# Summing the convolution taps of the first two blocks on TensorE, and taking the first unit's weights first

## Chip, cores and metric

The kernel runs on one core of one Trainium2 chip. The metric is the device time of one execution in microseconds. The kernel before was run three times: 1166.29, 1167.04 and 1167.16 us, median 1167.04 us.

## The reference

```python
# x [2, 4096, 192], weight_gen [2, 4096, 8, 7]; everything in fp32
w = softmax(weight_gen, axis=-1)                 # 7 taps for each token and head
x_pad = concat([zeros(B, 6, D), x], axis=1)
out[b, s, h, g] = sum_k w[b, s, h, k] * x_pad[b, s + k, h, g]     # h: 8 heads of 24 columns
y = out.reshape(8192, 192)
h = y @ moe_w_in;   y = maximum(0.01 * h, h) @ moe_w_out           # [192, 2048], [2048, 192]
h = y @ moe2_w_in;  y = where(h > 0, h, exp(min(h, 0)) - 1) @ moe2_w_out
```

## The kernel before

The 8192 tokens are cut into 16 blocks of 512. For each block three stages follow one another: a causal convolution with softmax weights (`conv_block`), a first feed-forward layer (l = 0) and a second (l = 1). Each layer has 2048 hidden columns, worked on as 8 **units** of 256. Of a unit, `ins` multiplies the block by 256 columns of the first weight matrix into a PSUM tile `h` (two buffers), `elementwise` makes the activation and splits it into a high part `gh` and a low part `gl` (ACT and DVE), and `outs`, four units later (LAG = 4), adds its product with the second weight matrix into the PSUM tile `acc`. All operands of the large matmuls are pairs of a high and a low part in fp32r, so every product is three matmuls. The two halves of the rows (0 to 63, 64 to 127) of TensorE are given separate matmuls, which run side by side.

Blocks 0 and 1 take turns, so the first four units are unit 0 of block 0, unit 0 of block 1, unit 1 of block 0 and unit 1 of block 1. These four only have their `ins` (`whole`, 9 steps of TensorE: 6 matmuls over all rows and 3 pairs); from the fifth unit on, one task `both` issues the `ins` of a unit and the `outs` of the unit four before it, and so on to the end.

The weights are made on the chip from 64-bit words (`split`): a DMA brings a piece (`load`, L213), ACT makes two intermediate values (`fraction`, L217, and `unbias`, L221), DVE joins them (`bits`, L228 and L231; `add`, L238), ACT writes the high part (`high`, L241) and DVE the low part (`low`, L246). Each unit needs its own pieces before its matmuls can start.

The convolution of one block: DMAs bring its weights (`load_w`, L288) and its tokens (`load_x`, L291). DVE and ACT make the softmax (`top`, `exp`, `total`, `scale`, L298 to L311). DVE then makes 7 products of tokens and weights (`mult`, L331, 128x768 each) and adds six of them to the first (`add`, L339). ACT writes the last 64 columns of each token twice (`double`, L374), TensorE transposes the block by matmuls with the identity (`transpose`, L388, 16 matmuls of 64x64), ACT writes the high part of the transposed block (L393) and DVE the low part (L396): that tile, `yt` or `xt`, is what the units multiply.

The order of every engine's work is fixed when the program is built. Each piece of work is a `Task` with a cost on one engine and a key; `Plan.order` plays the tasks through and, whenever an engine is free, gives it the ready task with the smallest key. Keys are counted in units of the steady run. The convolution of block 0 has an early key (`hurry` takes 12 off), and the first weights have the key of the unit that needs them. On the chip each engine then works its list off strictly in order.

Of the kernel before, what the change touches and what calls it, by code (L numbers as in the profile page):

```python
# [8 lines left out]
F32 = mybir.dt.float32  # L9
F32R = mybir.dt.float32r  # L10
I32 = mybir.dt.int32
U32 = mybir.dt.uint32
I64 = mybir.dt.int64
AF = mybir.ActivationFunctionType
ALU = mybir.AluOpType
AX = mybir.AxisListType

P = 128
D = 192
DFF = 2048  # L20
H = 8
K = 7
G = D // H
# [3 lines left out]
BS = 4  # L27
NB = SP // BS
N = BS * P
# [9 lines left out]

PACE = 0.28  # L40


# [88 lines left out]
def conv_moe_kernel(ctx: ExitStack, tc: tile.TileContext, x, wg, wi0, wi1, wo, out):  # L131
    nc = tc.nc

    rings = {
        "xs": (2, [P, BS + PAD, D], F32), "ws": (2, [P, BS * H, K], F32),
        "st": (1, [P, BS * H, 3], F32), "a": (1, [P, BS, D], F32), "prod": (1, [P, BS * D], F32),
        "xt": (1, [P, 4, N], F32R), "yt": (2, [P, 4, N], F32R),
        "h": (2, [P, 2, N], F32), "w": (3, [P, 2 * N], F32),
        "gh": (4, [P, 2 * N], F32R), "gl": (4, [P, 2 * N], F32R),
        "c": (1, [P, N], F32), "o": (1, [P, N], F32),  # L140
        "raw": (3, [P, 512], I64), "t": (2, [P, 512], I32),
    }
# [6 lines left out]
    plan = Plan({r: bufs for r, (bufs, _, _) in rings.items()})  # L149
# [18 lines left out]
    ident = const.tile([P, P], F32, name="ident")  # L168
    spare = const.tile([P, 1], F32, name="spare")
    win = {}  # L170
# [15 lines left out]
    bank = {p: acc[n % 2] for n, p in enumerate(phases)}  # L186
# [74 lines left out]
    def first(l, u):  # L261
        return min(at[l, i, u] for i in range(2))

    def split_in(l, part, m0, m1):
        c = slice(m0 // 2 * P, m1 // 2 * P) if part else slice(m0 * P, m1 * P)
        lo = [(win[l, part, 1][:, c], slice(None))]
        names = [("in", l, u) for u in range(m0 // 2, m1 // 2)]
        src = (wi0, wi1)[part][l][:, c]
        split(src, win[l, part, 0][:, c], lo, first(l, m0 // 2), names)

# [7 lines left out]
    xts = {}  # L278
    stored = {}

    def conv_block(i, due):
# [38 lines left out]
        prod = Slot("prod")  # L320
# [19 lines left out]

        y = [t, lx]
        for k in range(K):
            key = due - 0.8 - PACE * 2 * (K - 1 - k)
            takes = [[a], [prod]][k] if k < 2 else []
            uses = [r for r in [xs, ws, a] + [prod] * (k > 0) if r not in takes]
            y = [plan.add({"d": 0.95}, key, lambda k=k: mult(k), y, takes, uses)]
            if k:
                y = [plan.add({"d": 0.95}, key, add, y, uses=[a, prod])]
        last = y

        x_t = Slot("yt" if i < 2 else "xt")
        xts[0, i] = x_t

        place = Slot("h") if i == 2 else None

        def at_place():
            return place.tile if place else bank[0, i]

        def parts(j):

            return at_place()[:, :, j * N // 2 : (j + 1) * N // 2]

        def slot(j):
            return x_t.tile[:, j, :].rearrange("p (a b) -> p a b", a=2)

# [23 lines left out]

        def high(j):  # L390
            if not j:
                new(x_t)
            return nc.scalar.activation(slot(2 * j), parts(j), AF.Copy).ins  # L393

        def low(j):
            return nc.vector.tensor_tensor(  # L396
                out=slot(2 * j + 1), in0=parts(j), in1=slot(2 * j).bitcast(F32), op=ALU.subtract
            ).ins

        n = phases.index((0, i))  # L400
# [4 lines left out]

        k = due + (0.3 if i < 3 else 1.35)
        b = plan.add({"a": 0.55}, k, lambda: high(0), [t], [x_t], p)
        c = plan.add({"a": 0.55}, k + 0.1, lambda: high(1), [b], uses=[x_t] + p)
        b = plan.add({"d": 0.66}, k + 0.2, lambda: low(0), [b], uses=[x_t] + p)
        c = plan.add({"d": 0.66}, k + 0.3, lambda: low(1), [c], uses=[x_t] + p)  # L410
        return [b, c]

# [373 lines left out]
```

## Time and profile before

| | |
|---|---|
| median of 3 runs | 1167.04 us (1166.29 to 1167.16) |
| the profiled execution, its time | 1164.52 us |
| the profiled execution, its span | 1162.7 us |
| TensorE (PE) busy | 1119.4 us, 96% of the span |
| VectorE (DVE) busy | 808.2 us, 70% |
| ScalarE (ACT) busy | 788.3 us, 68% |
| PE busy in the first 52.43 us | 15.43 us |

The span is the part of the execution that the hardware profiler shows; the execution's own time is 1.8 us longer. Times in the views are counted from the start of the span. PE is the matmul row of TensorE, PEld its weight loads, POOL is GpSimd, SP the engine whose queue issues all DMAs. A busy PE is not a PE at its peak, since matmuls overlap each other.

### The profile page before, as it was taken

The numbers are of one execution on the slowest core, as the hardware profiler recorded it, in microseconds if no ns is written. First come the engines' busy times: TensorE is split into PE (matmuls) and PEld (weight loads), VectorE is DVE, ScalarE is ACT, GpSimd is POOL, SyncE is SP. The second block draws the span as 40 slices with busy tenths as digits, with TensorE's granted clock in tenths as the row PEclk, the third lists the DMA queues.
The fourth block names the chain that finished last, engine by engine and source line by source line (L and its number), as shares of the span: only waits on it lengthen the run. The fifth ranks groups of instructions, "written<-read, shape, count | busy, mean of one in ns | idle before, by whom it ended". The sixth has DMA issues, their size and how long they took to land.

```text
span 1162.7 us, 23771 instructions
## 1 busy us (share of the span) xinstructions
PE 1119.4 (96%) x9920; PEld 930.9 (80%) x9920; DVE 808.2 (70%) x1050; ACT 788.3 (68%) x1022; POOL 0.7 (0%) x6
## 2 busy tenths in 40 slices
PE   0699999999999999999999999999999999999998
PEld 0488998888888888888888888888888888888886
DVE  8999998948568494865948578494865839464464
ACT  1687898658586675857658576675857657585675
POOL 0000000000000000000000000000000000000000
PEclk9999999999999999999999999999999999999999
DMA  3424230000101001010100101001010000000000
GB/s 136 147 87 127 76 94 15 19 35 2 52 1 52 2 1 52 1 53 2 52 1 1 53 1 52 1 1 53 1 53 1 15 1 1 15 2 15 1 1 28
DMA packets 12620, 37.97 MB, mean 33 GB/s; under 512 B 1504, under 2 KB 3680, under 8 KB 12512
## 3 DMA queue, kind: packets, MB, share of 16 engines
q1 hardware_dynamic: 12512, 36.44, 9.8%
q8 instruction: 78, 1.28, 0.5%
q14 instruction: 30, 0.25, 0.1%
HBM read 30.15 MB, written 6.29 MB: 31 GB/s over the span
## 4 chain that ended last, share of the span: by engine, by line
PE 96%; DVE 3%; DMA 0%; ACT 0%; issue 0%; ACTq 0%; SPq 0%; DVEq 0%
PE acc L630 50%; PE h L630 45%; DVE prod L331 1%; DVE a L339 1%; PE acc L388 1%; DMA xs<-x_in 0%; ACT w L552 0%; DVE a L331 0%; DVE yt L396 0%; DVE t L231 0%; DVE w L563 0%; ACT yt L393 0%; DVE t L228 0%; DVE yt L440 0%; DVE c L425 0%
## 5 line engine op out<-in xcount | busy, mean ns | idle before, releaser
L630 PE MATMUL acc<-gh,wout 64*128 64x512 f32 (+1 forms) x3048 | 972.7, 386 | 0.0
L630 PE MATMUL acc<-gl,wout 64*128 64x512 f32 (+1 forms) x2032 | 785.5, 387 | 0.0
L630 PE MATMUL h<-yt,win 64*128 64x512 f32 (+1 forms) x2568 | 612.6, 389 | 18.5 <-ACT win L241 14.2
L630 PEld LDWEIGHTS acc<-gh,wout 64*128 64x128 f32 (+1 forms) x3048 | 560.1, 184 | 57.3
L630 PEld LDWEIGHTS h<-yt,win 64*128 64x128 f32 (+1 forms) x2568 | 470.2, 185 | 69.7 <-ACT win L241 14.3
L630 PE MATMUL h<-xt,win 64*128 64x512 f32 x2016 | 476.7, 386 | 0.1
L572 DVE TENSOR_TENSOR gl<-w,gh 128x1024 fp32r<-128x1024 f32 (+1 forms) x257 | 312.2, 1220 | 162.6 <-ACT gh L569 161.9
L630 PEld LDWEIGHTS acc<-gl,wout 64*128 64x128 f32 (+1 forms) x2032 | 374.1, 184 | 38.7 <-issue 0.4
L630 PEld LDWEIGHTS h<-xt,win 64*128 64x128 f32 x2016 | 370.6, 184 | 38.9 <-ACT gh L569 0.5
L569 ACT ACTIVATE gh<-w 128x1024 fp32r<-128x1024 f32 (+1 forms) x257 | 268.0, 1049 | 2.9
L552 ACT ACTIVATE w<-h 128x1024 f32<-128x1024 f32 x128 | 131.5, 1027 | 200.9 <-PE h L630 198.5
L563 DVE SCALAR_TENSOR_TENSOR w<-w,h 128x512 f32<-128x512 f32 x256 | 164.2, 683 | 141.4 <-ACT w L559 141.4
L555 ACT ACTIVATE w<-h 128x1024 f32<-128x1024 f32 x129 | 131.2, 1018 | 121.2 <-PE h L630 120.9
L559 ACT ACTIVATE w<-w 128x512 f32<-128x512 f32 x256 | 147.7, 624 | 3.9
L331 DVE TENSOR_TENSOR prod<-xs,ws 128x768 f32<-128x768 f32 x96 | 91.7, 955 | 1.9
L339 DVE TENSOR_TENSOR a<-a,prod 128x768 f32<-128x768 f32 x96 | 91.7, 955 | 1.5
L425 DVE TENSOR_TENSOR c<-acc,c 128x512 f32<-128x512 f32 (+1 forms) x32 | 22.0, 687 | 32.4 <-ACT o L455 23.6
L388 PE MATMUL acc<-ident,o 64*128 64x64 f32 x120 | 6.5, 231 | 19.6 <-ACT o L374 19.6
L388 PEld LDWEIGHTS acc<-ident,o 64*128 64x128 f32 x120 | 6.4, 147 | 21.6 <-issue 19.8
L418 ACT ACTIVATE c<-acc 64x512 f32<-64x512 f32 x32 | 19.1, 596 | 6.1 <-PE acc L630 5.2
L217 ACT ACTIVATE raw<-raw 128x384 int32<-128x384 uint32 (+3 forms) x30 | 17.2, 572 | 8.0 <-DMA raw<-wi_in 6.1
L231 DVE SCALAR_TENSOR_TENSOR t<-raw,t 128x384 int32<-128x384 int32 (+3 forms) x30 | 17.6, 585 | 1.0
(43 smaller groups left out, 257.8 us busy)
## 6 DMA issues: line engine op xcount, KB each, us to landing
xs<-x_in SPq DMA_DIRECT2D x16, 960.0 KB, 4.9
raw<-wo_in SPq DMA_DIRECT2D x16, 384.0 KB, 3.2
raw<-wi_in SPq DMA_DIRECT2D x10, 512.0 KB, 3.8
out_t<-o SPq DMA_DIRECT2D x16, 256.0 KB, 3.6
out_t<-c SPq DMA_DIRECT2D x16, 128.0 KB, 3.2
ws<-wg_in SPq DMA_DIRECT2D x16, 112.0 KB, 2.1
raw<-wi_in SPq DMA_DIRECT2D x2, 256.0 KB, 6.7
raw<-wi_in SPq DMA_DIRECT2D x1, 384.0 KB, 2.7
```

What stands on the lines that cost most here:

```text
L331: nc.vector.tensor_tensor(out=prods() if k else sums(), in0=xs.tile[:, k : BS + k, :].rearrange("p s (h g) -> p (s h) g", g=G), in1=ws.til ...
L339: nc.vector.tensor_tensor(out=sums(), in0=sums(), in1=prods(), op=ALU.add)
L388: nc.tensor.transpose(at_place()[:, half, c : c + 64], src, ident[r, r])
L418: nc.scalar.activation(new(c)[0:64], B[64:P], AF.Copy)
L425: nc.vector.tensor_tensor(out=c.tile[0:n], in0=B[0:n], in1=c.tile[0:n], op=ALU.add)
L552: nc.scalar.activation(cols(w), flat(), AF.Prelu, alpha=0.01)
L555: nc.scalar.activation(cols(w), flat(), AF.Relu, scale=-1.0)
L559: nc.scalar.activation(c, c, AF.Exp, scale=-1.0)
L563: nc.vector.scalar_tensor_tensor(out=c, in0=c, scalar=1.0, in1=h.tile[:, j, :], op0=ALU.subtract, op1=ALU.max,)
L569: nc.scalar.activation(cols(gh), cols(w), AF.Copy)
L572: return nc.vector.tensor_tensor(out=cols(gl), in0=cols(w), in1=cols(gh).bitcast(F32), op=ALU.subtract).ins
L630: i = nc.tensor.matmul(out_ap, w, x_ap, start=start, stop=stop).ins
```

## The change

For blocks 0 and 1 (ADDED = 2) the six additions on DVE, the doubling of the sum and the transposes of the sum are gone. Instead DVE writes each of the 7 products to a buffer of its own (`prod`, now 3 buffers), ACT writes the last 64 columns of each product twice (`dup`, 2 buffers), and TensorE multiplies every product by the identity in plain fp32 matmuls (not transposes) that accumulate over the 7 taps in PSUM: 16 matmuls for each tap, 112 for each block, 224 in all in place of 32 transposes. The high and low parts are then taken from PSUM as before (`splits`). Blocks 2 to 15 are computed as before.

The pieces of the first unit's first weight matrix get the key FIRST = -20.15, which places them ahead of the first block's products. The buffers for intermediate weights (`t`) go from 2 to 3. The scratch for DMAs described on the chip is set to 1024 bytes; no DMA of this kernel uses it.

```diff
-        "st": (1, [P, BS * H, 3], F32), "a": (1, [P, BS, D], F32), "prod": (1, [P, BS * D], F32),
+        "st": (1, [P, BS * H, 3], F32), "a": (1, [P, BS, D], F32), "prod": (3, [P, BS * D], F32),
...
-        "c": (1, [P, N], F32), "o": (1, [P, N], F32),
-        "raw": (3, [P, 512], I64), "t": (2, [P, 512], I32),
+        "dup": (2, [P, N], F32), "c": (1, [P, N], F32), "o": (1, [P, N], F32),
+        "raw": (3, [P, 512], I64), "t": (3, [P, 512], I32),
...
-        split(src, win[l, part, 0][:, c], lo, first(l, m0 // 2), names)
+
+        key = first(l, m0 // 2) if (l, m0) != (0, 0) else FIRST
+        split(src, win[l, part, 0][:, c], lo, key, names)
...
+        if i < ADDED:
+
+
+            def product(k, tap):
+                nc.vector.tensor_tensor(
+                    out=new(tap).rearrange("p (a g) -> p a g", g=G),
+                    in0=xs.tile[:, k : BS + k, :].rearrange("p s (h g) -> p (s h) g", g=G),
+                    in1=ws.tile[:, :, k : k + 1].to_broadcast([P, BS * H, G]),
+                    op=ALU.mult,
+                )
+
+            def doubled(tap, dup):
+                v = tap.tile.rearrange("p (s d) -> p s d", d=D)[:, :, P:D]
+                src = v.unsqueeze(2).to_broadcast([P, BS, 2, P // 2])
+                dst = new(dup).rearrange("p (s a b) -> p s a b", s=BS, a=2)
+                nc.scalar.activation(dst, src, AF.Copy)
+
+            def added(k, tap, dup):
+                for j in range(2):
+                    for s in range(BS):
+                        for half in range(2):
+                            r = slice(64 * half, 64 * half + 64)
+                            src = tap.tile[r, s * D : s * D + P]
+                            if j:
+                                src = dup.tile[r, s * P : (s + 1) * P]
+                            c = (j * BS + s) * 64
+                            nc.tensor.matmul(
+                                at_place()[:, half, c : c + 64], src, ident[r, r],
+                                start=k == j == s == 0,
+                                stop=(k, j, s) == (K - 1, 1, BS - 1),
+                            )
+
+            t = []
+            for k in range(K):
+                tap, dup = Slot("prod"), Slot("dup")
+                key = due - 0.8 - PACE * 2 * (K - 1 - k)
+                y = [plan.add({"d": 0.95}, key, lambda k=k, b=tap: product(k, b), y, [tap], [xs, ws])]
+                u = plan.add(
+                    {"a": 0.62}, key, lambda b=tap, d=dup: doubled(b, d), y, [dup], [tap]
+                )
+                t = [
+                    plan.add(
+                        {"pe": 1.2}, key, lambda k=k, b=tap, d=dup: added(k, b, d), [u] + t,
+                        uses=[tap, dup],
+                    )
+                ]
+            return splits(t[0], due + 0.3, [])
```

In the changed program the lines named above are L217 (load), L221 and L225 (fraction, unbias), L232 and L235 (bits), L242 (add), L245 (high), L250 (low), L304 to L317 (softmax), L361 and L364 (high and low part of the block), L383 (product), L394 (doubled), L405 (added), L610 to L630 (elementwise) and L688 (the units' matmuls).

The queue of DMAs (SP) is changed at its start: the two pieces for the first unit (256 and 128 columns) now stand directly behind block 0's softmax weights and ahead of block 0's tokens. Before, they stood behind the tokens of both blocks.

The rows below are in each engine's fixed order.

**VectorE (DVE), the first unit's weights.** Before, they stand inside block 1's convolution, around its last product (`a_105` is block 1's sum here):

```order
L331 TENSOR_TENSOR prod_109<-xs,ws 128x768
L339 TENSOR_TENSOR a_105<-a_105,prod_109 128x768
L228 TENSOR_SCALAR t<-t 128x128
L231 SCALAR_TENSOR_TENSOR t<-raw,t 128x128
L238 ISA t<-raw,t 128x512
L331 TENSOR_TENSOR prod_109<-xs,ws 128x768
L238 ISA t<-raw,t 128x256
L339 TENSOR_TENSOR a_105<-a_105,prod_109 128x768
L246 TENSOR_TENSOR win_71<-t,win_69 128x256
L246 TENSOR_TENSOR win_72<-t,win_70 128x128
```

Now they stand at the head of DVE's list, between the two halves of block 0's softmax:

```order
L232 TENSOR_SCALAR t<-t 128x256
L235 SCALAR_TENSOR_TENSOR t<-raw,t 128x256
L232 TENSOR_SCALAR t<-t 128x128
L235 SCALAR_TENSOR_TENSOR t<-raw,t 128x128
L242 ISA t<-raw,t 128x512
L242 ISA t<-raw,t 128x256
L312 TENSOR_REDUCE st_97<-ws 128x32
L313 TENSOR_SCALAR st_97<-st_97 128x32
L314 RECIPROCAL st_97<-st_97 128x32
L250 TENSOR_TENSOR win_71<-t,win_69 128x256
L250 TENSOR_TENSOR win_72<-t,win_70 128x128
L317 TENSOR_TENSOR ws<-ws,st_97 128x224
```

Everything that DVE does for the first unit's weights has moved from behind nearly all of both convolutions to ahead of block 0's first product.

**VectorE (DVE) around the low part of block 0** (`yt<-acc_79`), now; the first row is block 0's seventh product, the products behind it are block 1's:

```order
L383 TENSOR_TENSOR prod<-xs,ws 128x768
L317 TENSOR_TENSOR ws<-ws,st_97 128x224
L383 TENSOR_TENSOR prod<-xs,ws 128x768
L232 TENSOR_SCALAR t<-t 128x384
L235 SCALAR_TENSOR_TENSOR t<-raw,t 128x384
L383 TENSOR_TENSOR prod<-xs,ws 128x768 x2
L364 TENSOR_TENSOR yt<-acc_79,yt 128x512 x2
L383 TENSOR_TENSOR prod<-xs,ws 128x768 x3
```

Before, one product of block 1 stood ahead of the low part of block 0; now three stand there, and a piece of the second unit's weights.

**TensorE (PE) from block 0's last tap to the first unit** (`acc_79` is block 0's accumulator, `acc_80` block 1's; `h_366` is the first unit). Before, the transposes of block 0 stood directly ahead of the first unit:

```order
L388 MATMUL acc_79<-ident,o_139 128x64 x8
L388 MATMUL acc_79<-ident,a_105 128x64 x8
L630 MATMUL h_203<-yt,win_69 128x512
L630 MATMUL h_203<-yt,win_71 128x512
L630 MATMUL h_203<-yt,win_69 128x512 x2
```

Now:

```order
L405 MATMUL acc_79<-ident,prod 128x64 x8
L405 MATMUL acc_79<-ident,dup 128x64 x8
L405 MATMUL acc_80<-ident,prod 128x64 x8
L405 MATMUL acc_80<-ident,dup 128x64 x8
L405 MATMUL acc_80<-ident,prod 128x64 x8
L405 MATMUL acc_80<-ident,dup 128x64 x8
L405 MATMUL acc_80<-ident,prod 128x64 x8
L405 MATMUL acc_80<-ident,dup 128x64 x8
L688 MATMUL h_366<-yt,win_69 128x512
L688 MATMUL h_366<-yt,win_71 128x512
```

Three of block 1's seven taps stand between block 0's last tap and the first unit; the other four stand behind the first unit and ahead of the second.

## Rows read from the trace of the kernel before

**Rows 1.** The page: shares of the chain that ended last, by engine.

```profile
PE 96%; DVE 3%; DMA 0%; ACT 0%; issue 0%; ACTq 0%; SPq 0%; DVEq 0%
```

**Rows 2.** Stretches: start:end length, busy us (instructions) by engine, granted clock, DMA share, GB/s.

```profile
0.00:52.43 52.43, 15.43 (x81) 10.03 (x82) 45.95 (x78) 19.64 (x37) 0.70 (x6) 0.97 0.43 146
52.43:100.00 47.57, 47.57 (x426) 39.27 (x424) 44.71 (x70) 37.99 (x54) 0.00 (x0) 1.00 0.35 110
...
206.00:1157.60 951.60, 951.55 (x8496) 786.02 (x8492) 618.82 (x744) 637.39 (x796) 0.00 (x0) 1.00 0.06 19
```

**Rows 3.** PE's waits over the span: total us, times, longest us.

```profile
PE acc L388 <- ACT o L374: 19.6, 1, 19.6
PE h L630 <- ACT win L241: 14.2, 1, 14.2
```

**Rows 4.** Order of time, 0 to 24 us: start us, us, engine, instructions.

```profile
6.04 0.96 DVE L331 TENSOR_TENSOR a<-xs,ws 128x768 f32<-128x768 f32 x1 [0.42 <-DMA xs<-x_in]
...
9.33 0.44 ACT L217 ACTIVATE raw<-raw 128x256 int32<-128x256 uint32 x1 [5.17 <-DMA raw<-wi_in]
...
18.83 0.63 ACT L374 ACTIVATE o<-a 128x512 f32<-128x512 f32 x1 [8.00 <-DVE a L339]
...
19.60 0.69 PE L388 MATMUL acc<-ident,o 64*128 64x64 f32 x8 [19.60 <-ACT o L374]
...
20.76 1.09 ACT L393 ACTIVATE yt<-acc 128x512 fp32r<-128x512 f32 x2 [0.81 <-PE acc L388]
...
22.49 1.28 DVE L396 TENSOR_TENSOR yt<-acc,yt 128x512 fp32r<-128x512 f32 x2
```

**Rows 5.** The same view, 36 to 53 us.

```profile
36.70 4.08 PE L630 MATMUL h<-yt,win 128*128 128x512 f32 x11 [1.03 <-DVE win L246]
...
43.60 9.22 PE L630 MATMUL h<-yt,win 128*128 128x512 f32 x37 [2.21 <-DVE yt L396]
...
52.43 0.39 PE L630 MATMUL acc<-gl,wout 64*128 64x512 f32 x1
```

**Rows 6.** Groups by line and form, 0 to 52 us: count | busy us, mean ns.

```profile
L339 DVE TENSOR_TENSOR a<-a,prod 128x768 f32<-128x768 f32 x12 | 11.5, 958 | 0.4
...
L572 DVE TENSOR_TENSOR gl<-w,gh 128x1024 fp32r<-128x1024 f32 x2 | 2.4, 1218 | 0.2 <-ACT gh L569 0.2
...
L231 DVE SCALAR_TENSOR_TENSOR t<-raw,t 128x512 int32<-128x512 int32 x1 | 0.7, 691 | 0.0
```

**Rows 7.** Groups by line, DVE, 19.3 to 37 us: the first unit's pieces.

```profile
L231 DVE SCALAR_TENSOR_TENSOR t<-raw,t 128x256 int32<-128x256 int32 (+1 forms) x2 | 0.7, 360 | 0.1
L238 DVE CUSTOM_DVE_ANT_0 t<-raw,t 128x512 uint16<-128x512 uint16 (+1 forms) x2 | 0.7, 351 | 0.0
L246 DVE TENSOR_TENSOR win<-t,win 128x256 fp32r<-128x256 f32 (+1 forms) x2 | 0.6, 352 | 0.0
L228 DVE TENSOR_SCALAR t<-t 128x256 int32<-128x256 int32 (+1 forms) x2 | 0.5, 253 | 0.0
```

**Rows 8.** Stretches, DVE alone: start:end length, busy us (instructions), clock, DMA.

```profile
18.82:21.55 2.73, 2.53 (x8) 1.00 0.93 288
37.45:40.50 3.05, 2.91 (x9) 1.00 0.95 341
```

**Rows 9.** PE in order of time around block 3's transposes, 205.5 to 206.8 us.

```profile
205.66 0.39 PE L630 MATMUL acc<-gh,wout 64*128 64x512 f32 x1
...
205.89 0.41 PE L388 MATMUL acc<-ident,o 64*128 64x64 f32 x8
...
206.36 0.47 PE L630 MATMUL h<-yt,win 64*128 64x512 f32 x1
```

**Rows 10.** Stretches of 1 us, columns as in rows 2; the clock is the seventh column.

```profile
45.00:46.00 1.00, 1.00 (x5) 0.35 (x3) 0.96 (x3) 1.00 (x2) 0.00 (x0) 0.50 0.02 9
...
48.00:49.00 1.00, 1.00 (x6) 0.66 (x4) 0.97 (x3) 0.97 (x2) 0.00 (x0) 1.00 0.58 234
```

**Rows 11.** Matmuls of L630 in 37.8 to 38.8 us: duration ns min/median/max.

```profile
L630 PE MATMUL h<-yt,win x4: 628/628/628, 37.3 to 38.6; 128*128 128x512 f32 x4
```

More of the change, by code (lines that the diff above doesn't have):

```diff
@@ L40 @@
 PACE = 0.28
+FIRST = -20.15
+ADDED = 2
 class Task:
@@ L341, in conv_block, with parts, slot, high @@
         y = [t, lx]
+        x_t = Slot("yt" if i < 2 else "xt")
+        xts[0, i] = x_t
+        def parts(j):
+            return at_place()[:, :, j * N // 2 : (j + 1) * N // 2]
+        def slot(j):
+            return x_t.tile[:, j, :].rearrange("p (a b) -> p a b", a=2)
+        def high(j):
+            if not j:
+                new(x_t)
+            return nc.scalar.activation(slot(2 * j), parts(j), AF.Copy).ins
+        def low(j):
+            return nc.vector.tensor_tensor(
+                out=slot(2 * j + 1), in0=parts(j), in1=slot(2 * j).bitcast(F32), op=ALU.subtract
+            ).ins
@@ new lines, in splits, with at_place @@
+        def splits(t, k, p):
+            b = plan.add({"a": 0.55}, k, lambda: high(0), [t], [x_t], p)
+            c = plan.add({"a": 0.55}, k + 0.1, lambda: high(1), [b], uses=[x_t] + p)
+            b = plan.add({"d": 0.66}, k + 0.2, lambda: low(0), [b], uses=[x_t] + p)
+            c = plan.add({"d": 0.66}, k + 0.3, lambda: low(1), [c], uses=[x_t] + p)
+            return [b, c]
+        def at_place():
+            return place.tile if place else bank[0, i]
+        place = None
+        if i < ADDED:
[40 more added lines that the diff above has]
+            return splits(t[0], due + 0.3, [])
@@ L349, in conv_block @@
         last = y
-        x_t = Slot("yt" if i < 2 else "xt")
-        xts[0, i] = x_t
         place = Slot("h") if i == 2 else None
[L356 to L364, printed above, removed]
         twice = Slot("o")
@@ L388, in transpose @@
                         nc.tensor.transpose(at_place()[:, half, c : c + 64], src, ident[r, r])
[L390 to L398, printed above, removed]
         n = phases.index((0, i))
@@ L406, in conv_block @@
         k = due + (0.3 if i < 3 else 1.35)
[L407 to L411, printed above, removed]
+        return splits(t, k, p)
     def evac(l, i, after, key):
@@ L772 @@
     arrays = {k: np.ascontiguousarray(v) for k, v in arrays.items()}
-    nc = bacc.Bacc("TRN2", target_bir_lowering=False, num_devices=1)
+    nc = bacc.Bacc(
+        "TRN2", target_bir_lowering=False, num_devices=1, dynamic_dma_scratch_size=1024
+    )
     args = [
```

## Prediction

> **What bounds the kernel now.** I read the page's chain first: 96% of it is TensorE (PE) [rows 1]. The stretches then show that this holds from 52.43 us on and not before. From 206 us on PE is busy for 951.55 of 951.60 us, and from 52.43 to 100 us for all of 47.57; but in the first 52.43 us it is busy for 15.43 only, while VectorE (DVE) is busy for 45.95 [rows 2]. PE's work from the first `both` on is the same in both programs and has no gaps to win. So the time is the moment at which the steady run begins, 52.43 us [rows 5], plus a constant, and the question is by how much the change moves that moment.
>
> What sets it now is DVE's list. PE's two long waits are 19.6 us for block 0's doubled sum and then 14.2 us for the first unit's weights [rows 3]. The second is the telling one: block 0 is transposed and its low part is written by 23.8 us (1.28 from 22.49) [rows 4], yet the first unit starts in earnest at 36.70 [rows 5], because its weights stand in DVE's list behind nearly all of block 1's convolution. Their pieces were also late at ACT, at 9.33 us, behind the tokens of two blocks [rows 4].
>
> **The change, part by part.** I follow DVE's new list, with durations from the rows, up to the low part of block 1, which releases the second unit.
>
> *Weights first.* On DVE the first unit's pieces are two instructions each of four kinds, 0.7 + 0.7 + 0.6 + 0.5 = 2.5 us [rows 7]; with about 0.3 us of waiting for ACT in between they push block 0's first product from 6.04 us [rows 4] to 8.85. Block 0's tokens are issued behind two more DMAs, 0.9 us later, and share the engines with 0.39 MB more, another 1.2 us at the 341 GB/s of the second stretch of rows 8; they were there just before 6.04 us, so they come by 8.2 us, and these 2.8 us of DVE work hide that. If the cover were gone it would cost 2 us.
>
> *Six additions fewer, for each of two blocks.* 12 x 0.958 us of work [rows 6], 0.99 us each with the step to the next: 11.9 us less on DVE. Block 0's seven products then take 6.95 us, but block 1's softmax and one piece of the second unit's weights now stand between them (2.73 us in the stretch where they stand alone [rows 8], of which 2.4 ahead of the seventh product). The seventh ends at 8.85 + 6.95 + 2.4 = 18.2 us; before, the sum ended at 18.8, where the doubling starts [rows 4]. So block 0's convolution itself gains almost nothing.
>
> *Block 0's parts.* Behind the seventh product DVE has the rest of that softmax (0.4), three products of block 1 (2.97) and two steps of a weight piece (0.95), to 22.5, then the low part, 1.28 [rows 4]: 23.8 us, the same as before. The doubling (0.63), the last tap and the high part (1.09) [rows 4] fit ahead of it: 18.2 + 0.63 + 1.3 + 1.09 is 21.4 with handovers.
>
> *The first unit.* On PE three taps of block 1 stand ahead of it. The third product ends at 22.5, its doubling at 23.2, its tap at 24.5. The unit starts at 24.5 and not at 36.70, since its weights have been ready since 8.5 us: 12 us earlier, but PE now waits for block 1, not for weights.
>
> *Block 1.* Between the two low parts DVE has four products (3.96), seven steps of the second unit's first pieces (3.6: nine such steps, some of them on smaller pieces, fill 3.05 us in the second stretch of rows 8), the start of block 2's softmax (0.8), the low part of the first unit's result (1.22) and one larger piece (0.69 + 0.42) [rows 6]: 10.7 us. With the low part itself, 1.3, the second unit starts at 23.8 + 10.7 + 1.3 = 35.8 us; before, at 43.60 [rows 5]. That is 7.8 us.
>
> *The price of a tap.* No row shows a plain fp32 matmul. The nearest are the transposes by the same identity, of the same 64x64 shape: 16 of them take 206.36 - 205.89 = 0.47 us in the steady run, and 16 took 1.1 us from 19.60 to the high part's start, when PE had been idle [rows 9, 4]. Below stands 0.47 us, if a plain matmul costs what a transpose costs; above, four times the slow ones, 4.4. The columns alone do not explain 0.47: a pair of 512 columns takes 205.89 - 205.66 = 0.23 us [rows 9], so 8 pairs of 64 stream in 0.23 us, and the other half must be weight loads. If streaming is done four times and weights are loaded twice, side by side, that is about 1 us; one after the other, about 1.9. I take 1.3 us at full clock, nearer to the steady transposes because taps come one upon the other. Up to about 1.35 us the value does not matter, since products and doublings come no faster. Above it PE sets the pace: 14 taps in a row from 10.6 us, the first unit (2.05 us), 2.1 us for block 1's parts and the 8.83 us of the next three units reach 52.43 at a tap of 2.06 us. From there each 0.1 us costs 1.4.
>
> Here a rule of the Trainium skill speaks against the change. "FP8 and Floating Point Precision", section Matmul Precision, says that true fp32 takes four passes through the array. No run here shows it yet; by it a tap, estimated as four sets of transposes, is 1.9 us and the sum below would be nearly nothing; it is the second rival.
>
> *The clock.* The first unit before ran with matmuls of 628 ns [rows 11], as in the stretch from 45 to 46 us with a granted clock of 0.50, which is 1.2 GHz; at 48 us, after several us without a gap, it is 1.00, 2.4 GHz [rows 10]. I take the first two taps at half speed, 2.6 us each. That makes block 0's last tap 2 us late, but most of it vanishes behind DVE's three products; with a slot of `prod` freed late it leaves 0.9 us at block 1. The three units behind the second wait I leave at what they took before, 52.43 - 43.60 = 8.83 us [rows 5]: before as now PE idles over 2 us ahead of them and the clock then falls for some us.
>
> *ACT* gets 14 doublings for 2, 12 x 0.63 = 7.6 us more, in a stretch where it is busy for 19.64 of 52.43 us [rows 2, 4]; only the last one, behind the first unit's high part, lies on the chain, and it is in the times above. *The scratch size* costs nothing: no queue of POOL issues a DMA. *The third `t` buffer* lets ACT start a piece earlier; I count nothing for it.
>
> *Afterwards.* From 52.43 to 100 us DVE is busy for 44.71 of 47.57 us [rows 2], so it could be the next bound. But its list becomes 11.9 us shorter and PE asks only 7 us earlier: it arrives with some 5 us to spare. I count neither gain nor loss.
>
> **The sum.** -7.8 + 0.9 = -6.9, taken as -7.0 us: the steady run begins at 45.4 us. Against the profiled execution's own 1164.52 us that is 1157.5. That execution lies 2.5 us under the median of the three runs; the forecast is the median less the same difference, 1167.04 - 7.0 = **1160.0 us**. Chance 0.48.
>
> **The rivals.**
> *First, TensorE becomes the bound of the start and the kernel slower (0.12).* The clock stays at half during the taps, as it was for the first unit and as the slow transposes at 19.60 us suggest [rows 4, 11], and a tap costs two sets of slow transposes, 2.2 us. Then 10.6 + 14 x 2.2 + 4.1 + 2.1 + 8.83 = 56.4 us: 4 us late, 1171. It decides from 1.9 us per tap on (with the first unit at half clock). For it speaks that every tap waits for ACT's doubling, so PE has small gaps; against it, that slow taps would leave no gaps, and before, the clock rose after about 4 us without one.
> *Second, four passes (0.12).* A tap costs 4 x 0.47 = 1.9 us, and the first two 4.4: 10.6 + 8.8 + 12 x 1.9 + 2.05 + 2.1 + 8.83 = 55.2, 2.8 us late, 1169.8; with full clock from the first tap on it would be 2.2 us early, 1164.8. The page named above says so; against it speaks that half of a transpose's time is weight loads.
> *Third, the clock stays full (0.20).* PE has had taps to do for 25 us, the gap ahead of the second unit is short, and three units take 6.1 instead of 8.83 us: 0.9 + 2.7 us more, -10.6, 1156.4.
> *Fourth, the change wins its start and loses it again (0.08):* units come 7 us earlier, weight pieces do not, since the ring of three `raw` buffers and DMA hold them; waits of some 6 us appear between 50 and 180 us: 1166.
>
> **The numbers.** About 0.2%, 2.3 us, is what a measurement of this kernel can tell from no change. Faster by more: forecast, third rival and 0.03 of the second, 0.71. Within: the fourth and part of the second, 0.12. Slower: the first and the rest of the second, 0.17. The range goes from the third rival's time with a margin, 1155.5, to 1170.5, which takes in the four-pass case and leaves out half-clock taps and worse, under 0.2 in all.
>
> **What would show it.** First product near 8.9 us, first unit near 24.5, low part of block 1 near 36, first `outs` near 45.5. A tap under 1.4 us with gaps between taps means DVE and ACT set the pace; taps back to back from 10 to 40 us mean the first or second rival, and the granted clock in that stretch tells which. PE waits of more than 2 us after 50 us would be the fourth. If the first unit still waits for its weights, the move did not do what it says.

## The result and the profile after

The change made the kernel slower: 1178.59 us (median of 4 runs, 1178.39 to 1179.25) against 1166.67 (4 runs, 1166.29 to 1167.16), a ratio of 1.0103, 95% interval 1.0085 to 1.012. The forecast was 1160.0 us with a range from 1155.5 to 1170.5; the time lies 8 us above the range.

The page of the changed kernel (span 1176.6 us): the chain that ended last by engine and by line (against [rows 1]), and the groups of the taps (count | busy us, mean ns | idle before, releaser).

```profile
PE 98%; DMA 1%; ACT 1%; DVE 0%; issue 0%; SPq 0%; ACTq 0%; DVEq 0%
PE acc L688 49%; PE h L688 45%; PE acc L405 4%; DMA xs<-x_in 1%; PE acc L460 1%; ACT w L610 0%; ACT c L476 0%; DVE prod L383 0%; ACT gh L627 0%; SPq L217 0%; DVE yt L364 0%; DVE c L483 0%; ACTq L839 0%; ACT yt L361 0%; ACT yt L494 0%
...
L405 PE MATMUL acc<-ident,prod 64*128 64x64 f32 x224 | 23.8, 376 | 11.1 <-DVE prod L383 11.1
...
L383 DVE TENSOR_TENSOR prod<-xs,ws 128x768 f32<-128x768 f32 x14 | 13.2, 956 | 20.2 <-PE acc L405 18.6
L394 ACT ACTIVATE dup<-prod 128x512 f32<-128x512 f32 x14 | 8.8, 630 | 25.1 <-PE acc L405 11.9
```

The 3% that DVE had of the chain in [rows 1] is gone, and the taps (L405) have 4%. The last two rows turn the forecast round: it had DVE's products set the pace of the taps, but the products wait for the taps (18.6 us for a free buffer of `prod`), and the doublings wait 11.9 us for them.

The stretches of the changed kernel, columns as in [rows 2], cut at its own first `both`:

```profile
0.00:66.94 66.94, 53.89 (x496) 49.65 (x498) 36.73 (x73) 28.92 (x53) 0.70 (x6) 0.97 0.39 129
...
206.00:1171.50 965.50, 965.38 (x8618) 827.37 (x8614) 629.06 (x759) 648.34 (x812) 0.00 (x0) 1.00 0.06 19
...
30.00:40.00 10.00, 10.00 (x97) 10.00 (x96) 4.08 (x5) 2.86 (x5) 0.00 (x0) 1.00 0.01 2
...
59.00:60.00 1.00, 1.00 (x4) 0.71 (x4) 1.00 (x4) 0.73 (x2) 0.00 (x0) 0.50 0.07 16
...
62.00:63.00 1.00, 1.00 (x6) 0.79 (x5) 0.95 (x2) 0.80 (x1) 0.00 (x0) 1.00 0.51 111
```

PE's work in the start has grown from 15.43 us to 53.89, DVE's has fallen from 45.95 to 36.73. The steady run begins at 66.94 us instead of 52.43, 14.5 us late. What follows is the same: 1176.6 - 66.94 = 1109.7 us now, 1162.7 - 52.43 = 1110.3 before. So the spans differ by 13.9 us; the medians by 11.9, because the profiled execution of before lies 2.1 us under its median here and that of the change 0.2 us.

PE's waits over the span (total us, times, longest) and the chain that ended last up to 60 us (start us, us, what):

```profile
PE acc L405 <- DVE prod L383: 11.1, 1, 11.1
PE h L688 <- DVE yt L364: 1.9, 1, 1.9
PE h L688 <- ACT w L610: 0.6, 1, 0.6
```

```profile
2.12 7.83 DMA xs<-x_in
...
10.04 0.97 DVE prod L383
...
11.15 34.40 PE acc L405 x320
45.55 3.56 PE h L688 x12
49.10 7.11 PE acc L405 x128
```

The 19.6 and 14.2 us of waiting in [rows 3] are gone. In their place the chain lies on TensorE without a break for 45 us: 10 taps in 34.40 us, the first unit, 4 taps in 7.11. (A plain fp32 matmul leaves two MATMUL and two LDWEIGHTS records, so x320 are 160 matmuls, 10 taps of 16.) A tap costs 3.4 us in the first stretch and 1.8 in the second. The matmuls of L405 in either stretch, duration in ns min/median/max:

```profile
L405 PE MATMUL acc<-ident,dup x150: 417/418/418, 13.7 to 44.9; 64*128 64x64 f32 x150
L405 PEld LDWEIGHTS acc<-ident,dup x149: 329/330/331, 13.8 to 45.0; 64*128 64x128 f32 x149
...
L405 PEld LDWEIGHTS acc<-ident,prod x64: 184/188/189, 48.7 to 55.0; 64*128 64x128 f32 x64
L405 PE MATMUL acc<-ident,prod x64: 213/272/273, 48.9 to 55.0; 64*128 64x64 f32 x64
```

The same instruction takes 418 and 272 ns, its weight load 330 and 188: the first stretch runs at half clock. (`e_tokens` below shows the same 3.41 us for a tap under a column of 0.50.) In the change the granted-clock column does not say so: it reads 1.00 from 30 to 40 us, and up to its first fall at 58 us (the mean of 0.97 above is therefore too high). The first unit's own matmuls show the rise: 628 ns at 45.5 us, as in [rows 11], and 386 to 392 (least and median) from 48.1 us on.

The order of time on PE (start us, us, instructions; a row of x16 is half a tap):

```profile
12.88 1.95 PE L405 MATMUL acc<-ident,dup 64*128 64x64 f32 x16
...
43.60 1.95 PE L405 MATMUL acc<-ident,dup 64*128 64x64 f32 x16
45.48 3.63 PE L688 MATMUL h<-yt,win 128*128 128x512 f32 x12
...
58.10 9.24 PE L688 MATMUL h<-yt,win 128*128 128x512 f32 x37 [1.90 <-DVE yt L364]
66.94 0.39 PE L688 MATMUL acc<-gl,wout 64*128 64x512 f32 x1
```

From 12.88 to 43.60 us are nine taps, 3.41 us each. The sum of the start is then 11.15 + 10 x 3.41 = 45.3 for the first unit (45.48), 3.5 for it, 4 x 1.79 for the last taps, 1.9 for block 1's parts (58.10) and 8.84 for three units: 66.94.

Of the five runs of one kernel below (`e_fill`), one took 1176.98 us at a mean granted clock of 0.983 and is left out of its median and ratio, while runs of `e_tokens` and `e_all` at 0.984 to 0.987 are counted in theirs.

### The profile page after: what moved, and what is told of

The parts are those of the page before. It is cut to its first block, busy times and chain, and to the rows that moved or that the text cites. A ratio compares the mean times of both kernels' runs of the same rounds, so it can differ in the third digit from the quotient of the medians.

```text
span 1176.6 us, 24633 instructions
## 1 busy us (share of the span) xinstructions
PE 1157.6 (98%) x10336; PEld 1001.3 (85%) x10336; DVE 796.4 (68%) x1038; ACT 796.2 (68%) x1034; POOL 0.7 (0%) x6
## 4 chain that ended last, share of the span: by engine, by line
PE 98%; DMA 1%; ACT 1%; DVE 0%; issue 0%; SPq 0%; ACTq 0%; DVEq 0%
PE acc L688 49%; PE h L688 45%; PE acc L405 4%; DMA xs<-x_in 1%; PE acc L460 1%; ACT w L610 0%; ACT c L476 0%; DVE prod L383 0%; ACT gh L627 0%; SPq L217 0%; DVE yt L364 0%; DVE c L483 0%; ACTq L839 0%; ACT yt L361 0%; ACT yt L494 0%
## 5 line engine op out<-in xcount | busy, mean ns | idle before, releaser
L688 PE MATMUL acc<-gh,wout 64*128 64x512 f32 (+1 forms) x3048 | 971.6, 387 | 0.0
L688 PE MATMUL acc<-gl,wout 64*128 64x512 f32 (+1 forms) x2032 | 785.9, 387 | 0.0
L688 PE MATMUL h<-yt,win 64*128 64x512 f32 (+1 forms) x2568 | 610.3, 389 | 2.5 <-DVE yt L364 1.9
L688 PEld LDWEIGHTS acc<-gh,wout 64*128 64x128 f32 (+1 forms) x3048 | 560.8, 184 | 47.6
L688 PEld LDWEIGHTS h<-yt,win 64*128 64x128 f32 (+1 forms) x2568 | 470.7, 185 | 45.0 <-DVE yt L364 2.0
L688 PE MATMUL h<-xt,win 64*128 64x512 f32 x2016 | 476.0, 387 | 0.1
L630 DVE TENSOR_TENSOR gl<-w,gh 128x1024 fp32r<-128x1024 f32 (+1 forms) x257 | 312.3, 1220 | 165.7 <-ACT gh L627 165.1
L688 PEld LDWEIGHTS acc<-gl,wout 64*128 64x128 f32 (+1 forms) x2032 | 374.8, 184 | 32.2 <-issue 0.4
L688 PEld LDWEIGHTS h<-xt,win 64*128 64x128 f32 x2016 | 371.3, 184 | 32.1 <-ACT wout L245 0.5
L610 ACT ACTIVATE w<-h 128x1024 f32<-128x1024 f32 x128 | 131.5, 1027 | 202.5 <-PE h L688 202.2
L345 DVE TENSOR_TENSOR a<-a,prod 128x768 f32<-128x768 f32 x84 | 80.2, 954 | 1.1
L405 PE MATMUL acc<-ident,prod 64*128 64x64 f32 x224 | 23.8, 376 | 11.1 <-DVE prod L383 11.1
L405 PEld LDWEIGHTS acc<-ident,prod 64*128 64x128 f32 x224 | 22.6, 289 | 11.2 <-issue 11.1
L383 DVE TENSOR_TENSOR prod<-xs,ws 128x768 f32<-128x768 f32 x14 | 13.2, 956 | 20.2 <-PE acc L405 18.6
L394 ACT ACTIVATE dup<-prod 128x512 f32<-128x512 f32 x14 | 8.8, 630 | 25.1 <-PE acc L405 11.9
L405 PE MATMUL acc<-ident,dup 64*128 64x64 f32 x224 | 23.8, 376 | 0.0
```

Source lines behind the costliest of these rows:

```text
L345: nc.vector.tensor_tensor(out=sums(), in0=sums(), in1=prods(), op=ALU.add)
L383: nc.vector.tensor_tensor(out=new(tap).rearrange("p (a g) -> p a g", g=G), in0=xs.tile[:, k : BS + k, :].rearrange("p s (h g) -> p (s h) g ...
L405: nc.tensor.matmul(at_place()[:, half, c : c + 64], src, ident[r, r], start=k == j == s == 0, stop=(k, j, s) == (K - 1, 1, BS - 1),)
L610: nc.scalar.activation(cols(w), flat(), AF.Prelu, alpha=0.01)
L630: return nc.vector.tensor_tensor(out=cols(gl), in0=cols(w), in1=cols(gh).bitcast(F32), op=ALU.subtract).ins
L688: i = nc.tensor.matmul(out_ap, w, x_ap, start=start, stop=stop).ins
```

## The experiments

The theory: the taps run at half clock because nothing before them has raised it, and TensorE bounds the start. The rivals: a tap is too dear at either clock; or the moved weights and tokens, not the taps, cost the time. All ratios are to the kernel before, run on the same chip; the chips differ between groups of runs, so times of different groups are compared by their ratios.

**Each part of the change alone.** `e_first` keeps the weights first and puts no taps on TensorE:

```diff
-ADDED = 2
+ADDED = 0
```

> The weights of the first unit first, as in the change, but both convolutions summed on DVE as before. Theory 1 (TensorE's taps at half clock are the whole loss): DVE bounds the start again with the same instructions in another order, its first product comes at 10.0 us and not at 6.0 with 2.5 us of weight work already done; first `both` between 51 and 54 us (52.43 before), 1165 to 1168 us. Theory 2 (the weights ahead of block 0's tokens are the loss, since the tokens now land at 9.95 us, 4 us later): the start is late without any tap on TensorE too, first `both` at 56 us or later, 1170 us or more.

Measured: 1171.66 us (1169.03 to 1172.58, 4 runs), ratio 1.0055 (1.0038 to 1.0072). In order of time, PE:

```profile
26.91 4.50 PE L688 MATMUL h<-yt,win 128*128 128x512 f32 x12 [2.50 <-DVE yt L364]
...
43.23 9.12 PE L688 MATMUL h<-yt,win 128*128 128x512 f32 x37 [2.16 <-DVE yt L364]
51.96 0.41 PE L688 MATMUL acc<-gl,wout 64*128 64x512 f32 x1
```

The weights no longer hold the first unit, which starts at 26.91 instead of 36.70. But the second unit waits for block 1 and comes only 0.4 us earlier, and the first `both` 0.5 (51.96 against 52.43). The move alone is worth half a microsecond at the start, where the first theory had it (51 to 54 us); the time, 1165 to 1168 us by that theory, was missed. The 1170 us or more of the second theory fit the time, but not the start, which that theory put at 56 us or later. The profiled run is 4.5 us longer than that of before (and the fastest of the four), and PE's waits have a row that before has at 0.4 us:

```profile
PE h L688 <- DVE w L621: 4.8, 3, 3.3
```

It stands at 179 to 193 us. There DVE's list is the bound: from 182 to 190 us DVE is busy for 7.93 of 8.00 us, PE for 4.68 (before 7.28 and 8.00). `e_taps` has the like, the full change has not. Why this order of DVE's work comes out late there stays open; no run was made for it.

`e_taps` does the other part, with the first unit's weights where they were:

```diff
-        key = first(l, m0 // 2) if (l, m0) != (0, 0) else FIRST
+        key = first(l, m0 // 2)
```

> The taps on TensorE as in the change, the first unit's weights where they were before. Theory 1: taps start at about 7.1 us and run back to back at 3.41 us each; first `both` about 4 us earlier than the change's 66.94, at 63, 1174 to 1176 us, still slower than before. Theory 2: without the moved weights the taps' gain shows, 1164 us or less.

Measured: 1186.73 us (1184.72 to 1187.85, 4 runs), ratio 1.018 (1.0164 to 1.0195). PE in order of time:

```profile
7.29 1.97 PE L405 MATMUL acc<-ident,prod 64*128 64x64 f32 x16 [7.29 <-DVE prod L383]
...
53.39 1.95 PE L405 MATMUL acc<-ident,dup 64*128 64x64 f32 x16
55.27 11.95 PE L688 MATMUL h<-yt,win 128*128 128x512 f32 x48
...
67.65 0.49 PE L688 MATMUL acc<-gl,wout 64*128 64x512 f32 x1
```

All 14 taps stand ahead of the first unit and all are slow, from 7.29 to 55.1 us, 3.41 us each. So the first `both` comes at 67.65 us, not at the 63 that was expected: 0.7 us later than in the change, although the first tap comes 3.9 us earlier. It is the taps that cost the start, not the moved weights; these even help, because a first unit between the taps leaves the last four fast (4 x 1.62 = 6.5 us). Behind the first `both` 8.7 us more are lost (1186.0 - 67.65 = 1118.4 us against 1109.7), which puts the time above the expected 1174 to 1176; 5.1 of them are waits for DVE's `w`, as in `e_first`, and behind these the granted clock falls too (0.98 from 120 to 206 us).

**Cheap taps.** In `e_cheap` each matmul of a tap becomes a transpose, with the same instructions around it. It leaves out the sum over the taps, so it shows a time and is no kernel to use:

```diff
-                            nc.tensor.matmul(
-                                at_place()[:, half, c : c + 64], src, ident[r, r],
-                                start=k == j == s == 0,
-                                stop=(k, j, s) == (K - 1, 1, BS - 1),
-                            )
+                            nc.tensor.transpose(at_place()[:, half, c : c + 64], src, ident[r, r])
```

> Each tap as 16 transposes of the same tiles in place of 16 plain fp32 matmuls: the taps are not summed, only the last one is left in PSUM. All products, doublings, waits and orders stay. Theory 1: a tap costs 1.1 us at half clock and 0.47 at full, DVE and ACT set the pace, and the rest of the prediction's sum holds from a first product at 10.0 us: first `both` at 45 to 48 us, about 1161 us. Theory 2, or a loss in the handovers between DVE, ACT and TensorE: 1170 us or more.

Measured: 1155.05 us (1154.65 to 1155.45, 4 runs), ratio 0.991 (0.9895 to 0.9924).

```profile
11.74 0.64 PE L405 MATMUL acc<-ident,prod 64*128 64x64 f32 x8
...
12.61 0.64 PE L405 MATMUL acc<-ident,prod 64*128 64x64 f32 x8
14.11 0.69 PE L405 MATMUL acc<-ident,dup 64*128 64x64 f32 x8 [0.86 <-ACT dup L394]
...
23.48 3.07 PE L684 MATMUL h<-yt,win 128*128 128x512 f32 x12
26.39 0.41 PE L405 MATMUL acc<-ident,prod 64*128 64x64 f32 x8
...
26.89 0.41 PE L405 MATMUL acc<-ident,prod 64*128 64x64 f32 x8
...
43.12 0.39 PE L684 MATMUL acc<-gl,wout 64*128 64x512 f32 x1
```

With taps of 0.87 us (11.74 to 12.61) and later 0.50 (26.39 to 26.89) the gaps are back, DVE and ACT set the pace, and the steady run begins at 43.12, earlier than the 45 to 48 us expected. What DVE saves is real; the price of a tap on TensorE loses it. These transposes give the measure too: 3.41 / 0.87 is 3.9 before the first unit, 1.79 / 0.50 is 3.6 behind it (3.8 against the 0.47 of [rows 9]).

**Full clock for the same taps.** `e_warm` is the change with 26 matmuls of zeros ahead of the first tap, into an `h` buffer that is not yet in use:

```diff
+        idle = wout[1].rearrange("p m f -> p (m f)")[:, :N]
+        nc.gpsimd.memset(idle.bitcast(F32), 0.0)
+        for n in range(WARM):
+            nc.tensor.matmul(tiles[1][:, 0, :], idle[:, :P], idle, start=True, stop=True)
```

> The change, with 26 matmuls of 512 columns on zeros ahead of the first tap, in time in which TensorE waits (from about 2 to 10 us). Theory 1: the clock is full when the taps begin and a tap costs 1.79 us instead of 3.41; if it stays full through all taps, first `both` is at 49 us, 1160 to 1162 us; if taps alone do not hold it, it falls on the way and the first `both` lies between 49 and 67 us. Theory 2 and a loss in the handovers: no change, 1178 us.

Measured: 1159.76 us (1159.10 to 1160.58, 4 runs), ratio 0.995 (0.9936 to 0.9965).

```profile
1.82 8.19 PE L808 MATMUL h<-wout 128*128 128x512 f32 x26 [1.82 <-POOL wout L806]
10.76 1.11 PE L407 MATMUL acc<-ident,prod 64*128 64x64 f32 x16 [0.75 <-DVE prod L385]
11.70 1.06 PE L407 MATMUL acc<-ident,dup 64*128 64x64 f32 x16
...
27.78 1.06 PE L407 MATMUL acc<-ident,dup 64*128 64x64 f32 x16
28.77 2.55 PE L690 MATMUL h<-yt,win 128*128 128x512 f32 x12
...
40.33 9.27 PE L690 MATMUL h<-yt,win 128*128 128x512 f32 x37 [1.91 <-DVE yt L366]
49.21 0.39 PE L690 MATMUL acc<-gl,wout 64*128 64x512 f32 x1
```

The same taps now take (27.78 - 11.70) / 9 = 1.79 us each, and the first `both` comes at 49.21 instead of 66.94. The 17.7 us are 16.2 for ten taps, 1.0 for the first unit and 0.4 for an earlier first tap. This decides it: the taps, their order and the moved weights are those of the change, only the clock differs, and the kernel is about 18 us faster than the change (0.995 against 1.0103 of the time before) and faster than before. "A tap is too dear at either clock" falls. (Of the 6.3 us to the median of before, the profiled spans, 1158.8 and 1162.7, show 3.9: that execution of before lies 1.5 us under its median, that of `e_warm` 0.8 above.)

`e_bwarm` gives the kernel before the same help: 56 matmuls of zeros behind block 0's transposes and 8 ahead of the second unit.

```diff
+WARM = 56
+
+FILL = 8
```

> The kernel before, with the filling alone: 56 matmuls of 512 columns on zeros behind block 0's transposes, where TensorE waits 14 us, and 8 more in the 2.2 us wait ahead of the second unit. No tap on TensorE. If the gain of e_warm came from the clock of the first units and not from the taps, this gains as much, 1160 us. By theory 1 block 1's convolution on DVE still sets the start of the second unit at about 43.6 us, and only the units behind it run faster, 6.3 us instead of 8.8: first `both` at about 50 us, 1163 to 1165 us.

Measured: 1165.56 us (1163.77 to 1166.52, 10 runs), ratio 0.9992 (0.9983 to 1.0001): no gain that these runs can tell from none, and the first `both`, expected at about 50 us, came at 53.38.

```profile
36.94 2.33 PE L638 MATMUL h<-yt,win 128*128 128x512 f32 x11 [0.68 <-DVE win L250]
...
44.55 9.22 PE L638 MATMUL h<-yt,win 128*128 128x512 f32 x37 [2.74 <-DVE yt L404]
```

The second unit started at 44.55 us, 0.95 us later than before, behind a gap of 2.74 us, which 8 fillers did not close, so a full clock at the second unit was not put to the test here. The first unit did run at full clock, 2.33 us for 11 matmuls against 4.08 [rows 5], and nothing came of it, because the second unit waits for block 1.

`e_fill` adds 8 fillers ahead of the second unit to `e_warm`, where the clock fell to 0.50 behind a gap of 1.9 us:

```diff
+                if v.s == 1:
+                    idle = wout[1].rearrange("p m f -> p (m f)")[:, :N]
+                    for n in range(FILL):
+                        nc.tensor.matmul(v.h.tile[:, 0, :], idle[:, :P], idle, start=True, stop=True)
```

> e_warm with 8 more matmuls of 512 columns on zeros between the last tap and the second unit, where TensorE idles 2 us and the clock then is at 0.50 for 3 us. If it is the gap that lets the clock fall, the three units take 6.3 to 7 us instead of 8.9 and the time is 2 to 2.5 us under e_warm, 1157 to 1158 us. If it is the 26 us of narrow taps, the filling comes too late and nothing changes, 1160 us.

Measured: 1159.19 us (1159.04 to 1159.48), ratio 0.9941 (0.9928 to 0.9954).

```profile
40.42 7.53 PE L692 MATMUL h<-yt,win 128*128 128x512 f32 x36
47.78 0.39 PE L692 MATMUL acc<-gl,wout 64*128 64x512 f32 x1
```

Three units take 7.36 us instead of 8.88, and the steady run starts at 47.78, 1.4 us earlier. That is less than the 2 to 2.5 us expected, and the ratios show 1.0 us of it (0.995 and 0.9941). The run of 1176.98 us lies 17.8 us above the median of the others; half clock for ten taps and the first unit costs the change 17.2 us. Its mean clock of 0.983 over 1175.2 us stands for an estimated 40 us at 0.50, and ten such taps and a first unit last 34.1 + 3.5. So it is likely, though no trace of that run shows it, that the taps lost the clock there.

`e_close` has 29 warm-up matmuls for 26.

> The kernel of the warm-up and the eight fillers, with 29 warm-up matmuls in place of 26, which at 0.22 us each ends the warm-up near 10.75 us, directly ahead of the first tap at 10.84 us, where a gap of 0.73 us stood. If that gap was what let the clock fall in one of the five runs of that kernel (1176.98 us at a mean clock of 0.983), all runs are now alike, at 1159.2 us within 0.8, taps 1.79 us, first `both` at 47.8 us. If the clock falls at the taps for another reason, some runs come out at 1165 to 1178 us again. If 29 are too many, the first tap starts late by up to 0.5 us and the time is 1159.5.

Measured: 1159.31 us (1158.97 to 1159.89, 5 runs), ratio 0.9944 (0.9931 to 0.9958). The gap ahead of the first tap shrank to 0.44 us, not to nothing, because the clock rose earlier in the warm-up (the last matmul of 632 ns starts at 4.1 us, in `e_fill` at 5.4). All five runs agree. That fits the gap as the cause in that run of `e_fill`; five runs beside four of five don't prove it.

**Tokens first.** In `e_tokens` block 0's tokens go ahead of the weights (`FIRST = -20.1`), with 16 warm-up matmuls, so that the taps begin 3.5 us earlier. `e_all` adds the 8 fillers, `e_keep` six more behind the first half of the first tap, `e_each` one more in every later tap. Of the edit of `e_each`, without the warm-up and the 8 fillers:

```diff
-FIRST = -20.15
+FIRST = -20.1
...
+                    if j == 0:
+                        idle = wout[1].rearrange("p m f -> p (m f)")[:, :N]
+                        for _ in range(6 if (i, k) == (0, 0) else 1):
+                            nc.tensor.matmul(lasting["h"][0][1][:, 0, :], idle[:, :P], idle, start=True, stop=True)
```

> e_warm with block 0's tokens ahead of the first unit's weights in the DMA queue (key -20.1 instead of -20.15; DVE then makes two products first and the weights behind them) and 16 instead of 26 matmuls on zeros, since the taps can start sooner. The tokens land at 6 us, the first tap starts at 7.1 to 7.6 us instead of 10.76, and TensorE sets the pace with 14 taps of 1.79 us: 3 us under e_warm, about 1157 us. If DVE's list sets the pace, under 1 us.

> e_tokens and e_fill together: if each takes a place of its own on the chain, their gains add up to 4.5 to 5.5 us under e_warm, 1154 to 1156 us.

> e_all with 6 more matmuls of 512 columns on zeros behind the first half of the first tap, where e_tokens and e_all idled 1.3 us before their clock fell to 0.50. If a gap lets the clock fall and taps alone hold but do not raise it, all 14 taps now cost 1.79 us from 7.3 us on, and the time is 1154 to 1156 us in every run, without the spread of e_tokens (1159.8 to 1173.7). If the clock falls by itself during taps, the spread stays.

> e_keep with one more matmul of 512 columns in each later tap, between its halves. If TensorE sets the pace, 13 taps cost 0.22 to 0.25 us more each: 3 us over e_keep. If the taps lose the clock without them, it is faster than e_keep.

Measured: `e_tokens` 1164.67 us (12 runs, near 1159.8, 1164.5 and 1173.5), ratio 1.0007 (0.9982 to 1.0033); `e_all` 1168.11 (12 runs, 1162.74 to 1173.74), 1.0013 (0.9989 to 1.0037); `e_keep` 1161.76 (12 runs, 1158.85 to 1165.74), 0.9964 (0.9954 to 0.9975); `e_each` 1165.89 (10 runs, 1165.38 to 1166.07), 0.9996 (0.9987 to 1.0005). None came out at the time expected of it (1157, 1154 to 1156, 1154 to 1156, and 3 us over `e_keep`). In the profiled runs of `e_tokens` and `e_all` the gain of the earlier start is lost where the clock falls among the taps. Stretches of the profiled `e_tokens` run, columns as in [rows 2]:

```profile
8.00:10.00 2.00, 0.71 (x14) 0.57 (x13) 1.52 (x7) 1.43 (x4) 0.00 (x0) 1.00 0.98 400
...
12.00:14.00 2.00, 2.00 (x24) 2.00 (x22) 1.35 (x2) 1.26 (x3) 0.00 (x0) 0.53 0.81 286
...
35.00:40.00 5.00, 5.00 (x52) 5.00 (x50) 2.15 (x3) 0.63 (x1) 0.00 (x0) 0.50 0.02 3
```

The first tap's second half waits 1.29 us for ACT and starts at 9.66. The taps behind it run at full clock up to 12.1 us; from there the clock is at 0.50 and stays there through 28 us of taps, with PE busy all the time, until in the first unit (40.33 to 43.85) it rises. Here the column shows what the durations showed in the change: these slow taps take 3.41 us as well.

`e_keep` was to tell whether that gap lets the clock fall or the clock falls by itself during taps; by its own terms a spread that stays speaks for the second. It stayed, if smaller (6.9 us instead of 13.9 in `e_tokens`). But a gap stayed too, even in the profiled run, which kept the clock:

```profile
23.95 1.11 PE L409 MATMUL acc<-ident,dup 64*128 64x64 f32 x16 [0.81 <-ACT dup L398]
```

With that gap and six fillers its first unit starts at 28.57 us, where `e_close` has 28.56: the earlier first tap gains nothing there even at full clock. `e_each` closes nearly all gaps (0.5 us of waits are left at its taps) and its runs agree, but the fillers cost what they save, and they put matmuls of 512 columns among the taps. So what lets the clock fall among the taps, the gap or the taps themselves, stays open.

**Wide matmuls among cold taps.** `e_mixed` is the change without a warm-up, with two matmuls of zeros, 512 columns each, between the halves of every tap:

> The change as it is (weights first, no matmuls ahead of the taps), with 2 matmuls of 512 columns on zeros between the halves of each tap. If these do not raise the clock, each tap costs 3.41 + 0.86 us and the time is about 12 us over the change, 1190 us. If they raise it after some taps, a tap costs 2.2 us from then on and the time lies between 1163 and 1175 us.

Measured: 1195.28 us (1195.21 to 1195.91, 4 runs), ratio 1.025 (1.0237 to 1.0263).

```profile
12.74 1.22 PE L417 MATMUL h<-wout 128*128 128x512 f32 x2
...
56.73 1.97 PE L409 MATMUL acc<-ident,dup 64*128 64x64 f32 x16
58.63 4.29 PE L696 MATMUL h<-yt,win 128*128 128x512 f32 x12
```

That did not raise the clock either: ten taps of 4.8 us (4.3 expected), all slow up to the first unit, fast behind it.

The best version is the change with warm-up and fillers (`e_close`; `e_fill` with one run in five left out), 6.5 to 7 us under the kernel before and, by the ratios, 18 to 19 under the change.

## Why the prediction was wrong

*The step that failed* stands under "The clock": "I take the first two taps at half speed, 2.6 us each." Ten taps ran at half speed, all that stood ahead of the first unit, and they alone cost 10 x (3.41 - 1.79) = 16.2 us against the full clock. The reason given was that in the kernel before the clock was at 1.00 again after several us without a gap; but those were a unit's matmuls of 512 columns, and taps without a gap for 34 us did not do it.

*The price of a tap* was mis-sized: 1.3 us taken, 1.79 measured at full clock, inside the bounds of 0.47 and 4.4. The rule that the second rival was built on had the better number: "FP8 and Floating Point Precision", section Matmul Precision, of the Trainium skill says that true fp32 takes four passes, and the trace agrees, with 3.9 times a transpose of the same shape at half clock and 3.6 to 3.8 at full. The reason against it, that half of a transpose's time is weight loads, did not hold: the whole came out near four times. (A slip stands in that estimate: streaming four times and weights loaded twice, one after the other, is 4 x 0.23 + 2 x 0.24 = 1.4 us by its own numbers; its 1.9 is four whole transposes.) With 1.79, a full clock and the text's own formula, 10.6 + 14 x 1.79 + 2.05 + 2.1 + 8.83, the steady run begins at 48.6; `e_warm` shows 49.21. So this term alone would have left the kernel faster, near 1163 us and inside the range.

*The first rival* had the mechanism, half clock throughout and TensorE as the bound, but priced a tap at 2.2 us from two sets of slow transposes. With ten taps of 3.41 and four of 1.79 its own sum is 10.6 + 34.1 + 7.2 + 4.1 + 2.1 + 8.83 = 66.9, against 66.94 measured; the closeness is in part luck, since the first tap starts 0.55 us later than in that sum and the first unit is 0.65 us shorter. The rival ended 7.6 us short (1171). The argument that held it at 0.12, "slow taps would leave no gaps, and before, the clock rose after about 4 us without one", is the one that the trace refutes. The two rivals came true together, dear taps at half clock, and no sum of the prediction has both throughout. The sign that was to tell them apart, the granted clock from 10 to 40 us, reads 1.00 there and would have pointed to the second alone; the durations tell.

*Tokens.* They were to land by 8.2 us; they landed at 9.95, 7.83 us after their issue, and the first product came at 10.04 instead of 8.85. DVE's cover was gone, as the prediction allowed, for 1.5 us. The first tap, put at 10.6 us, started at 11.15: in a start that TensorE bounds, these 0.55 us count in full.

*What held.* The first unit does not wait for its weights (PE's waits above have no row for `win`). DVE's list is the shorter for the taps: with cheap ones the steady run begins at 43.12, where the forecast had 45.4. Behind the start there is neither gain nor loss (1109.7 and 1110.3 us), and the fourth rival's waits are not there (of PE's waits 0.6 us lie behind 60 us). The third rival's full clock ahead of the second unit did not come by itself: a gap of 1.9 us let it fall to 0.50 at 59 us; only the fillers of `e_fill` kept it, worth 1.5 us. That `e_warm` measured 1159.76 us, close to the forecast 1160.0, bears out neither its sum nor its mechanism: there TensorE bounds the start, which ends at 49.21 us and not at 45.4.

## What to carry to other kernels

Before work moves to TensorE, price it at the clock that it will find there: read what the engine did in the microseconds before, and take the price at both levels. In this kernel the taps did not raise the clock and 26 matmuls of zeros ahead of them did, which turned a loss of 1.0% against the kernel before into a gain of 0.5%. An addition moved to TensorE as plain fp32 matmuls cost 3.6 to 3.9 times the transposes of its shape here, 1.79 us for a tap at full clock against the 0.96 us of DVE's addition; it paid in a stretch where TensorE had been waiting, and no run tried it elsewhere.

## What the runs showed of the hardware

Small plain fp32 matmuls did not raise the clock, and mostly kept the level that they found. In the change 34 us of them, without a gap, began and ended at half clock, and in `e_tokens` 28 us of them, with 0.50 in the column; in `e_warm` the ten taps from 10.76 to 28.6 us stayed at full. The Trainium skill, "TensorE: Matmul & The Clock Gate", section Part 1: The HAM clock gate, says that "the default state is throttled, and activity releases the throttle"; for these taps the trace does not agree, for the warm-up and the first units it does.

The clock fell behind short gaps, and not behind every one: 1.9 us ahead of the second unit in the change and in `e_warm`, 2.74 us behind matmuls of 512 columns in `e_bwarm`, and 1.29 us in the profiled `e_tokens`, there only after 2.4 us more of taps at full clock. A gap of 0.81 us in the profiled `e_keep` (1158.91 us) did no harm. For the second unit `e_fill`, which fills the gap with matmuls of 512 columns and keeps the clock, shows the gap as the cause; among the taps that is not shown.

The granted-clock column reads 1.00 up to the first fall in the trace, at either level: in the change up to 58 us, in `e_warm` also under the first warm-up matmuls of 628 ns. In the first microseconds of a run the level is read from the durations: 628 or 389 ns for a matmul of 512 columns (both in the warm-up of `e_warm`), 418 or 272 for one of the taps' records.
